# Half-height transposes, 32-column memory products and reciprocal gates in a hand-scheduled segment-attention kernel

## The chip, the cores and the metric

The kernel runs on one core of a Trainium2 chip. The metric is the device time of one execution in microseconds, the median of several runs. The core has a matrix engine (TensorE, "PE" in the profile, its weight loads "PEld"), three elementwise engines (VectorE "DVE", ScalarE "ACT", GpSimd "POOL") and a queue that issues transfers (SyncE, "SP"). PE writes to PSUM, which has banks of 512 float32 a partition; POOL does not touch PSUM here.

## The reference

Per token, the output is a gate g times a segment attention with a compressive memory, plus (1 - g) times x, in which one single token of the sequence gets an FFN added.

```python
# S = 2048 tokens, D = 640, H = 32 heads of 20, 4 segments of L = 512
for s in range(N):
    qs, ks, vs = q[:, :, s], k[:, :, s], v[:, :, s]
    logits = jnp.einsum("bhqd,bhkd->bhqk", qs, ks) * scale + mask      # causal in the segment
    p = _softmax(logits, axis=-1)
    a_dot = jnp.einsum("bhqk,bhkd->bhqd", p, vs)
    pq = phi(qs)
    num = jnp.einsum("bhld,bhde->bhle", pq, M)
    den = jnp.einsum("bhld,bhd->bhl", pq, z)[..., None] + 1e-6
    o = g * (num / den) + (1.0 - g) * a_dot                            # g = sigmoid(beta), per head
    pk = phi(ks)
    M = M + jnp.einsum("bhld,bhle->bhde", pk, vs)
    z = z + jnp.einsum("bhld->bhd", pk)
a = o @ wo
...
return g_x * a + (1 - g_x) * (x + upd)     # g_x = sigmoid(x . gate_w); upd: FFN of the top token
```

## The kernel before

**Staging.** The 32 heads are handled in two halves of 16, each with four segments: eight units `u`. A unit has four groups of four heads, so there are 32 groups `n`. For a unit, five jobs project x to q and k (channels on partitions, jobs 0 to 2) and to v (tokens on partitions, jobs 3 and 4). To keep precision, each operand is a high and a low part, and three products are added. A job is `pair_up`: two PSUM banks are filled at once, one from rows 0 to 63 and one from rows 64 to 127 of the array ("pairs" of matmuls, line L390); in a second phase the two halves are exchanged, and between the phases PE is drained (`where` is then "swap").

**Attention.** q and k go through DRAM (`place`, `place_low`, `bring_back`; L483 and L487 make the high and low parts in rings `hi` and `lo` of two buffers) and come back as stacks `qs`, `ks`. `a_step` makes logits with queries on partitions (L726, mask L733 and L735) for their maxima (L743 on DVE); `b_step` makes them again with keys on partitions (L790), ACT takes the exponential (L794) and POOL the causal select (L800). `pv_step` multiplies with v, with a column of ones for the sum (L815), in four column tiles of 32, one per head; ACT copies the result out (L821). `norm` then transposes it back to tokens on partitions (L842, four transposes of 128x128), divides by the sum and multiplies by `ogate` (DVE, L845 to L848), adds the memory's part (POOL, L851) and stores the rows to DRAM (`otok`).

**Memory.** `memory_read` (L569) multiplies phi(q) of a group with a block matrix `mbd` (80x84), copies the result (ACT, L572), and divides and gates it (DVE L575, L576, POOL L578, L580); there are 24. `memory_write` (L593) makes the update, six times. `keys` (L558) transposes phi(k) in 64-row halves; `m_rows` (L770) transposes the maxima, one small transpose on each half.

**Output stage.** For each of 16 tiles of 128 tokens: `out_rows` loads the rows, transposes them (L1043, five transposes of 128x128 into two banks) and splits them (L1047, L1050), `pair_up` multiplies with `wo`, `out_mix` prepares the x part (ACT L1024 and L1027, POOL L1029), and L1112, L1116 and L1118 finish.

**Order.** Nothing is scheduled by the compiler. The kernel's main loop is a planner that keeps a clock for each engine (`now`), adds an assumed duration with each step (`run`, `pe`, `dma`) and emits the step that comes next. `turned` and `chores` are lists of steps that fit in between: `turn()` runs the first of `turned` when both spare banks are free, `visit()` runs chores, and the product of the next group. Of four banks, two belong to the running pair-up and two (`others()`) are lent out by `misc()`; `flip()` exchanges the pairs. `use(m)` notes the tiling mode of the array, and charges 0.22 us in the planner where it changes: `(64, 128)` for projections, logits, `keys` and `m_rows`, `(128, 32)` for the products with p and the FFN, `(128, 128)` for `norm`, `out_rows`, `memory_read` and `memory_write`. `held` counts, for each high and low copy, the transfers that are not issued yet; `parts_free` lets a next copy begin when the last but one has none left. In this document a "read" is one `memory_read`, an "update" one `memory_write`, and a "visit" a stretch in which PE leaves the 64-row mode and comes back.

## Time and profile before

| | us |
|---|---|
| median of 3 runs | 637.65 |
| lowest, highest | 634.68, 644.41 |
| the profiled execution | 641.31 |
| its span from first to last instruction | 639.6 |

The mean granted clock of PE over the span is 0.98. In the page, "busy" of PE is the union of modelled matmul durations, and these overlap: two matmuls on different halves of the array, or one behind another, lie over each other by part of their length. For what a matmul costs in a stream, the distance from its start to the next one's start is read in the timeline, not its duration. In the timeline a row is a group of like instructions (start, time from the first start to the last end, engine, line, operation, tiles, shapes, count); in the groups a row has count, then total busy time and the mean duration of one in ns, then idle time before. A row of the windows gives the stretch and its length, the busy time and count of PE, PEld, DVE, ACT and POOL, PE's granted clock, DMA's busy share and GB/s. A wait row gives who waited for whom, the total in us, how often, and the longest. A float32 matmul appears as two instructions (eight for the four of a read, 32 for the 16 of an update).

### The profile page before, as it was taken

To read this page: it belongs to the slowest core of one execution; us is meant where nothing else is said; L and a number is where in the kernel's file an instruction comes from. 1 tells how busy PE (TensorE), PEld (TensorE's weight loads), DVE (VectorE), ACT (ScalarE), POOL (GpSimd) and SP (SyncE) were. 2 spreads that over 40 slices of the span, in tenths; PEclk is the share of its full clock that TensorE was granted. 3 is DMA by queue.
4 is the path that set the end of the run, shared out by engine and by line. 5 is a ranking of instruction groups with operands and counts; after the bars stand their busy time and mean duration, and the time that the engine had idled before them with its cause. 6 is when DMAs were issued, how large, how long until landed. Compare 5 with 4: busy or idle time off the path is not lost.

```text
span 639.6 us, 17532 instructions
## 1 busy us (share of the span) xinstructions
PE 599.2 (94%) x7008; PEld 472.4 (74%) x7008; DVE 330.6 (52%) x536; ACT 395.8 (62%) x695; POOL 356.9 (56%) x484
## 2 busy tenths in 40 slices
PE   5998999989999998989999999999999889988996
PEld 4887877777678876767678677786687677766885
DVE  7422555556655545554557465565565565423221
ACT  8736466647667675656766567674666756664442
POOL 4646354544747686647655565664658554554333
PEclk8997999989999999999999999999999979999999
DMA  7797765435554289789868977867465943334451
GB/s 186 221 265 214 203 185 169 133 103 160 136 139 130 77 195 247 226 230 253 271 220 253 259 225 231 235 190 204 149 191 153 271 123 116 95 101 139 145 186 63
DMA packets 81320, 116.57 MB, mean 182 GB/s; under 512 B 36112, under 2 KB 41752, under 8 KB 81240
## 3 DMA queue, kind: packets, MB, share of 16 engines
q1 hardware_dynamic: 81240, 115.46, 62.6%
q8 instruction: 56, 0.92, 0.6%
q14 instruction: 24, 0.20, 0.1%
HBM read 72.94 MB, written 41.96 MB: 180 GB/s over the span
## 4 chain that ended last, share of the span: by engine, by line
PE 78%; DMA 5%; ACT 5%; POOL 3%; DVE 3%; issue 3%; SPq 2%; POOLq 0%; DVEq 0%; ACTq 0%
PE bank L390 41%; PE bank L815 11%; PE a L726 6%; PE bt L790 6%; PE bank L569 3%; PE bank L842 3%; PE bank L593 2%; SPq L151 2%; PE a L735 2%; DMA stkk<-lo 2%; DMA stkq<-hi 1%; PE bank L1043 1%; PE bank L948 1%; DMA ks<-stkk 1%; POOL xf L1029 1%
## 5 line engine op out<-in xcount | busy, mean ns | idle before, releaser
L743 DVE TENSOR_REDUCE mx<-a 128x2 f32<-128x768 f32 (+1 forms) x192 | 160.1, 862 | 111.8 <-PE a L733 59.9
L794 ACT ACTIVATE p<-bt 128x1024 f32<-128x1024 f32 x160 | 163.9, 1025 | 64.3 <-PE bt L790 62.0
L800 POOL TENSOR_SCALAR_AFFINE_SELECT p<-p 128x512 f32<-128x512 f32 (+1 forms) x160 | 87.6, 548 | 105.0 <-ACT p L794 90.0
L390 PE MATMUL bank<-xhi,whi 64*128 64x512 f32 (+1 forms) x480 | 101.7, 386 | 7.7 <-DVE ou L848 3.3
L390 PE MATMUL bank<-xhi,wlo 64*128 64x512 f32 (+1 forms) x480 | 100.6, 377 | 0.0
L390 PE MATMUL bank<-xlo,whi 64*128 64x512 f32 (+1 forms) x480 | 99.1, 371 | 0.6 <-POOL xlo L179 0.6
L790 PE MATMUL bt<-qs,ks 62*128 62x384 f32 (+3 forms) x512 | 74.0, 333 | 4.6 <-ACT p L794 4.6
L726 PE MATMUL a<-ks,qs 60*128 60x384 f32 (+3 forms) x512 | 73.5, 330 | 3.6 <-DMA ks<-stkk 2.5
L815 PE MATMUL bank<-p,va 128*32 128x512 f32 (+3 forms) x1024 | 75.6, 436 | 0.5 <-ACT half L1116 0.4
L390 PEld LDWEIGHTS bank<-xhi,whi 64*128 64x128 f32 x480 | 55.2, 192 | 17.4 <-issue 8.4
L508 POOL TENSOR_TENSOR phi<-phi,neg 128x512 f32<-128x512 f32 x38 | 49.3, 1298 | 24.6 <-ACT phi L506 23.8
L815 PEld LDWEIGHTS bank<-p,va 128*32 128x32 f32 x1024 | 30.0, 109 | 43.9 <-issue 31.0
L487 POOL TENSOR_TENSOR lo<-phi,hi 128x512 fp32r<-128x512 f32 x40 | 51.6, 1293 | 17.0 <-DMA stkk<-lo 16.4
L390 PE MATMUL bank<-whi,xhi 64*128 64x322 f32 (+1 forms) x320 | 58.5, 331 | 2.4 <-DVE fg L937 0.7
L790 PEld LDWEIGHTS bt<-qs,ks 62*128 62x128 f32 x512 | 49.8, 190 | 14.0 <-ACT p L794 5.7
L726 PEld LDWEIGHTS a<-ks,qs 60*128 60x128 f32 x512 | 47.9, 189 | 16.5 <-issue 6.9
L390 PE MATMUL bank<-whi,oh 64*128 64x320 f32 x320 | 52.0, 330 | 7.7 <-DVE ol L1050 6.0
L390 PEld LDWEIGHTS bank<-xlo,whi 64*128 64x128 f32 x480 | 55.8, 192 | 4.5 <-POOL xlo L179 1.0
L390 PEld LDWEIGHTS bank<-xhi,wlo 64*128 64x128 f32 x480 | 56.1, 193 | 3.2 <-issue 0.5
L390 PE MATMUL bank<-wlo,xhi 64*128 64x322 f32 (+1 forms) x320 | 57.2, 320 | 0.0
L390 PE MATMUL bank<-whi,xlo 64*128 64x322 f32 (+1 forms) x320 | 56.5, 315 | 0.0
L821 ACT COPY pvs<-bank 128x512 f32<-128x512 f32 x32 | 18.7, 586 | 58.3 <-PE bank L815 55.1
(121 smaller groups left out, 1142.7 us busy)
## 6 DMA issues: line engine op xcount, KB each, us to landing
qs<-stkq SPq DMA_DIRECT2D x64, 240.0 KB
ks<-stkk SPq DMA_DIRECT2D x64, 240.0 KB
raw<-in_xT_dram SPq DMA_DIRECT2D x40, 256.0 KB
stkq<-hi SPq DMA_DIRECT2D x32, 320.0 KB
stkq<-lo SPq DMA_DIRECT2D x32, 160.0 KB
otok<-ou SPq DMA_DIRECT2D x32, 160.0 KB
xf<-in_x_dram SPq DMA_DIRECT2D x8, 640.0 KB
out_dram<-xf SPq DMA_DIRECT2D x16, 320.0 KB
```

The costliest lines, as they stand in the source:

```text
L390: nc.tensor.matmul(o, a, b, start=phase == 0 and i == 0, stop=phase == 1 and i == n - 1)
L487: nc.gpsimd.tensor_tensor(out=lo, in0=c, in1=f32(hi), op=OP.subtract)
L508: nc.gpsimd.tensor_tensor(out=c, in0=c, in1=r, op=OP.add)
L569: nc.tensor.matmul(nm[:, c, :], e[:GC, 128 * c:128 * c + 128], mbd[:, g, :], start=True, stop=True)
L726: nc.tensor.matmul(a[:, b, at:at + w], q_, ks[n % NS][64 * b:64 * b + ST, p, :w], start=(i, p) == LOGITS[k][0][:2], stop=False)
L743: nc.vector.tensor_reduce(out=mx[n][:, :, p, i:i + 1], in_=a[:, :, at:at + w], axis=AX.X, op=OP.max)
L790: nc.tensor.matmul(bt[:, b, at:at + w], k_, qs[n % NS][64 * b:64 * b + ST + 2, p, L - w:], start=True, stop=True)
L794: nc.scalar.activation(pt, bt, AF.Exp, scale=SCALE)
L800: nc.gpsimd.affine_select(out=d, in_=d, pattern=[[0, e[1]] for e in dims[:-1]] + [[1, 128]], base=0, channel_multiplier=-1, compare_op=OP. ...
L815: nc.tensor.matmul(pv[32 * j:32 * j + 32, 128 * c:], va[u % 2][:, c, VW * h:VW * h + 32], pt_tiles[n, j % 2, c][:, j // 2], start=c == 0, ...
L821: nc.scalar.copy(pvs[n], pv)
L842: nc.tensor.transpose(tp[:, c].rearrange("p j r -> p (j r)"), o[:, 128 * c:128 * c + 128], identf)
```

## The change

- `norm` and `out_rows` transpose in halves of 64 rows into two banks, in mode `(64, 128)`. `norm` is put in `turned` and no longer into `chores`; the next product waits until it has been done.
- `memory_read` and `memory_write` are cut into tiles of 32 output partitions, in mode `(128, 32)`.
- `gate` holds 1 + exp(-beta) and `ogate` 1 + exp(beta), so that a multiplication comes before the one reciprocal.
- `out_mix` uses one DVE instruction where ACT and POOL had one each.
- A next high and low copy begins only when the transfers of the last but one are planned to have landed.
- 22 warm-up transposes stand at the start, 12 before.

```diff
-WARM = 12
+WARM = 22
...
-    held = []
+    held, held_at = [], {}
...
             held[k] -= 1
-            return fn()
+            held_at[k] = max(held_at.get(k, 0.0), fn())
...
     def parts_free():
-        return len(held) < 2 or held[-2] == 0
+        return len(held) < 2 or held[-2] == 0 and held_at[len(held) - 2] <= now["PE"] + 0.3
...
         def fn():
+            nc.scalar.activation(ogate, gate, AF.Exp)
             nc.scalar.activation(gate, gate, AF.Exp, scale=-1.0)
-            nc.vector.tensor_scalar(gate, gate, 1.0, None, op0=OP.add)
-            nc.vector.reciprocal(gate, gate)
-            nc.vector.tensor_scalar(ogate, gate, -1.0, 1.0, op0=OP.mult, op1=OP.add)
...
+            for t in (gate, ogate):
+                nc.scalar.activation(t, t, AF.Copy, bias=1.0)
...
     def memory_read(u, g, e):
-        use((128, 128))
+        use((128, 32))
...
         for c in range(4):
-            nc.tensor.matmul(nm[:, c, :], e[:GC, 128 * c:128 * c + 128], mbd[:, g, :], start=True, stop=True)
-        end = pe(0.6, mbd_at[0])
+            for r in range(0, 128, 32):
+                nc.tensor.matmul(nm[r:r + 32, c, :], e[:GC, 128 * c + r:128 * c + r + 32], mbd[:, g, :], start=True, stop=True)
+        end = pe(0.75, mbd_at[0])
+        rm = pool.tile([128, 4, 4], F32, tag="rm", bufs=2, name="rm")
+        nc.vector.scalar_tensor_tensor(out=rm, in0=nm.rearrange("p c (j e) -> p c j e", e=VW)[:, :, :, DH], scalar=1e-6,
+                                       in1=sub(gate, HH * (u // SEG) + 4 * g, [[0, 4], [1, 4]]), op0=OP.add, op1=OP.mult)
+        mid = run("DVE", 0.25, end)
         t = pool.tile([128, 4, 4, VW], F32, tag="num", bufs=RN, name="num")
         nc.scalar.copy(t.rearrange("p c j e -> p c (j e)"), nm)
-        end = misc_free[i] = run("ACT", 0.55, end)
-        rm = pool.tile([128, 4, 4], F32, tag="rm", bufs=2, name="rm")
-        nc.vector.tensor_scalar(rm, t[:, :, :, DH], 1e-6, None, op0=OP.add)
+        misc_free[i] = run("ACT", 0.55, mid)
         nc.vector.reciprocal(rm, rm)
-        end = run("DVE", 0.5, end)
-        nc.gpsimd.tensor_tensor(out=rm, in0=rm, in1=sub(gate, HH * (u // SEG) + 4 * g, [[0, 4], [1, 4]]), op=OP.mult)
+        end = run("DVE", 0.25)
...
     def memory_write(u):
-        use((128, 128))
+        use((128, 32))
...
             for c in range(4):
-                nc.tensor.matmul(mp[:, g, :], kk[:, g, c, :], va[u % 2][:, c, GW * g:GW * g + GW],
-                                 start=c == 0, stop=c == 3)
-        end = pe(2.3, va_at[0])
+                for r in range(0, GC, 32):
+                    p = slice(r, min(r + 32, GC))
+                    nc.tensor.matmul(mp[p, g, :], kk[:, g, c, p], va[u % 2][:, c, GW * g:GW * g + GW], start=c == 0, stop=c == 3)
+        end = pe(2.6, va_at[0])
...
-        chores.insert(0, (misc_free[i] + 0.1, 0.6, lambda: norm(n), lambda: True))
+        turned.append((misc_free[i] + 0.1, lambda: norm(n), lambda: True))
...
     def norm(n):
-        use((128, 128))
-        tp, i = misc([128, 4, 4, 32])
+        use((64, 128))
...
+        for r in range(2):
+            p = slice(64 * r, 64 * r + 64)
+            tp, i = misc([128, 4, 2, 32])
+            misc_free[i] += 1e6
+            two.append((tp, i, slice(2 * r, 2 * r + 2)))
         for c in range(4):
-            nc.tensor.transpose(tp[:, c].rearrange("p j r -> p (j r)"), o[:, 128 * c:128 * c + 128], identf)
-        end = pe(0.5)
-        rs = pool.tile([128, 4, 4], F32, tag="rs", bufs=2, name="rs")
-        nc.vector.reciprocal(rs, tp[:, :, :, DH])
-        nc.vector.tensor_tensor(out=rs, in0=rs, in1=sub(ogate, HH * hf + 4 * g, [[0, 4], [1, 4]]), op=OP.mult)
-        ou = pool.tile([128, 4, 4, DH], F32, tag="ou", bufs=2, name="ou")
-        nc.vector.tensor_tensor(out=ou, in0=tp[:, :, :, :DH], in1=sub(rs, 0, [[4, 4], [1, 4], [0, DH]]), op=OP.mult)
-        end = misc_free[i] = run("DVE", 1.0, end)
+            for r, (tp, i, h) in enumerate(two):
+                p = slice(64 * r, 64 * r + 64)
+                nc.tensor.transpose(tp[:, c].rearrange("p j r -> p (j r)"), o[p, 128 * c:128 * c + 128], identf[p, p])
+        end = pe(0.47)
+        for tp, i, h in two:
+            nc.vector.tensor_tensor(out=rs[:, :, h], in0=tp[:, :, :, DH], in1=sub(ogate, HH * hf + 4 * g + h.start, [[0, 4], [1, 2]]),
+                                    op=OP.mult)
+        nc.vector.reciprocal(rs, rs)
+        end = run("DVE", 0.6, end)
+        for tp, i, h in two:
+            nc.vector.tensor_tensor(out=ou[:, :, h], in0=tp[:, :, :, :DH], in1=sub(rs, h.start, [[4, 4], [1, 2], [0, DH]]), op=OP.mult)
+            end = misc_free[i] = run("DVE", 0.33)
...
     def out_mix(t):
...
-        row = pool.tile([128, D], F32, tag="raw", bufs=4, name="row")
-        nc.scalar.activation(row, R["yb"], AF.Copy, scale=R["oh"][:, t:t + 1])
-        end = run("ACT", 0.85)
-        nc.gpsimd.tensor_tensor(out=xf[t], in0=row, in1=xf[t], op=OP.add)
-        mixed[t] = run("POOL", 1.6, end)
+        nc.vector.scalar_tensor_tensor(out=xf[t], in0=R["yb"], scalar=R["oh"][:, t:t + 1], in1=xf[t], op0=OP.mult,
+                                       op1=OP.add)
+        mixed[t] = run("DVE", 0.9, end)
...
     def out_rows(t):
-        use((128, 128))
+        use((64, 128))
...
+        for k in range(KT):
+            for r, (tp, i) in enumerate(two):
+                p = slice(64 * r, 64 * r + 64)
+                nc.tensor.transpose(tp[:, k, :], src[k // 4][p, 128 * (k % 4):128 * (k % 4) + 128], identf[p, p])
+        done = pe(0.6, ot_at[t])
+        ready = []
+        for r, (tp, i) in enumerate(two):
+            h_, l_ = (v.rearrange("p (k t) -> p k t", k=KT)[:, :, 64 * r:64 * r + 64] for v in (hi, lo))
+            nc.scalar.copy(h_, tp)
+            end = run("ACT", 0.45, done)
+            nc.vector.tensor_tensor(out=l_, in0=tp, in1=f32(h_), op=OP.subtract)
+            misc_free[i] = run("DVE", 0.5, end)
+            ready = [end + 0.1, misc_free[i] + 0.1]
...
     def pv_ready(t):
-        return n < NG and done_b[0] > n and p_at[n] <= t and misc_ready() <= t
+        return n < NG and done_b[0] > n and n - 1 not in pvs and p_at[n] <= t and misc_ready() <= t
...
     def visit(budget, pv):
-        if pv:
-            if done_pv[0] - 1 in pvs:
-                chores.pop(0)[2]()
...
-        times += [mbd_at[0], step_at[0]] + ...
+        times += [mbd_at[0], step_at[0]] + list(held_at.values())[-2:] + ...
```

More of the change, by code (lines that the diff above doesn't have):

```diff
@@ L426, in fn @@
                 later_dma(end, lambda: bring_back(kind, m), 0.5)
+            return end
         from_part(ready, fn)
@@ L1038, in out_rows @@
         lo = pool.tile([128, D], F32R, tag="lo", bufs=2, name="ol")
-        ready = [], []
-        for k0, k1 in ((0, 4), (4, 5)):
-            tp, i = misc([128, 128 * (k1 - k0)])
-            for k in range(k0, k1):
-                nc.tensor.transpose(tp[:, 128 * (k - k0):128 * (k - k0) + 128], src[k // 4][:, 128 * (k % 4):128 * (k % 4) + 128],
-                                    identf)
-            end = pe(0.13 * (k1 - k0), ot_at[t])
-            c = slice(128 * k0, 128 * k1)
-            nc.scalar.copy(hi[:, c], tp)
-            end = run("ACT", 0.17 + (k1 - k0) / 10, end)
-            ready[0].append(end + 0.1)
-            nc.vector.tensor_tensor(out=lo[:, c], in0=tp, in1=f32(hi)[:, c], op=OP.subtract)
-            misc_free[i] = run("DVE", 0.17 + (k1 - k0) / 7.5, end)
-            ready[1].append(misc_free[i] + 0.1)
+        two = []
+        for r in range(2):
+            tp, i = misc([128, KT, 64])
+            misc_free[i] += 1e6
+            two.append((tp, i))
+        for k in range(KT):
[11 more added lines that the diff above has]
+            ready = [end + 0.1, misc_free[i] + 0.1]
         rowed[t] = hi, lo, ready
@@ L1094, in g @@
                     wh, wl = (v[p, n * b:n * b + n] for v in W["O", k])
-                    return ((h_, wh), (h_, wl), (l_, wh))[part] + (max(ready[part == 2][k == 4], need(("O", k))),)
+                    return ((h_, wh), (h_, wl), (l_, wh))[part] + (max(ready[part == 2], need(("O", k))),)
                 return g
```

10 lines of the change are left out of this document (6 added, 4 removed).

## The prediction

> **What bounds the kernel now.** I read the page first, then the PE timeline around single steps, then the groups and the waits.
>
> ```profile
> span 639.6 us, 17532 instructions
> ...
> PE 599.2 (94%) x7008; PEld 472.4 (74%) x7008; DVE 330.6 (52%) x536; ACT 395.8 (62%) x695; POOL 356.9 (56%) x484
> ...
> PE 78%; DMA 5%; ACT 5%; POOL 3%; DVE 3%; issue 3%; SPq 2%; POOLq 0%; DVEq 0%; ACTq 0%
> PE bank L390 41%; PE bank L815 11%; PE a L726 6%; PE bt L790 6%; PE bank L569 3%; PE bank L842 3%; PE bank L593 2%; SPq L151 2%; PE a L735 2%; DMA stkk<-lo 2%; DMA stkq<-hi 1%; PE bank L1043 1%; PE bank L948 1%; DMA ks<-stkk 1%; POOL xf L1029 1%
> ```
>
> TensorE works for 599.2 of 639.6 us, and 78% of the chain that ended last is its own work, spread over the projections (L390), the products with p (L815), the logits (L726, L790) and, smaller, the three things that the change rewrites: the memory product (L569), the transposes of norm (L842) and the memory update (L593). No other engine is above 62%. So a cut of PE's own time, anywhere, should shorten the run by about the chain's share of it, and work that is moved between ACT, DVE and POOL should matter little except at the end.
>
> **What a change of tiling costs.** The stream runs in 64-row tiles; whenever L842, L569, L593 or L1043 come, the whole array is used, and then the stream returns.
>
> ```profile
> 569.10 0.90 PE L390 MATMUL bank<-whi,ol 64*128 64x320 f32 x10
> 569.92 0.76 PE L1043 MATMUL bank<-identf,ot 128*128 128x128 f32 x5
> 570.62 0.50 PE L790 MATMUL bt<-qs,ks 62*128 62x384 f32 x4
> ...
> 613.22 0.91 PE L390 MATMUL bank<-whi,ol 64*128 64x320 f32 x10
> 614.05 0.77 PE L1043 MATMUL bank<-identf,ot 128*128 128x128 f32 x5
> 614.92 0.41 PE L390 MATMUL bank<-whi,oh 64*128 64x320 f32 x2
> ...
> 616.49 0.90 PE L390 MATMUL bank<-whi,ol 64*128 64x320 f32 x10
> 617.23 0.31 PE L390 MATMUL bank<-whi,oh 64*128 64x320 f32 x2
> ...
> 618.69 0.90 PE L390 MATMUL bank<-whi,ol 64*128 64x320 f32 x10
> 619.68 0.41 PE L390 MATMUL bank<-whi,oh 64*128 64x320 f32 x2
> 619.93 0.31 PE L390 MATMUL bank<-wlo,oh 64*128 64x320 f32 x2
> ...
> 123.09 2.55 PE L593 MATMUL bank<-va,kk 128*80 128x84 f32 x32
> 125.48 0.60 PE L842 MATMUL bank<-identf,pvs 128*128 128x128 f32 x4
> ...
> L842 PE MATMUL bank<-identf,pvs x128: 270/273/330, 94.8 to 584.7; 128*128 128x128 f32 x128
> ```
>
> Ten matmuls (five pairs) take 0.74 us from start to start (616.49 to 617.23), 0.15 a pair. A full transposition of 128x128 takes a step of (0.60 - 0.273) / 3 = 0.109 us. The visit at 569.92 takes 1.52 from the pairs' start to the next matmul; less 0.74 and 5 x 0.109 that leaves 0.24, and the first step after a change is some 0.10 longer (0.25 at 619.68 where 0.15 is usual): 0.34 a visit. Between a pair-up's two phases the code drains PE anyway: without a visit that costs 0.99 - 0.74 = 0.25 (618.69 to 619.68), with one 1.70 - 0.74 - 0.545 = 0.42, so a visit there costs only 0.17.
>
> **Part by part, on PE.**
>
> ```profile
> 107.65 0.22 PE L770 MATMUL bank<-identf,mneg 64*66 64x64 f32 x2
> 107.68 0.48 PE L390 MATMUL bank<-xlo,whi 64*128 64x512 f32 x2
> 107.99 0.39 PE L390 MATMUL bank<-xhi,whi 64*128 64x512 f32 x2
> 108.22 0.39 PE L390 MATMUL bank<-xhi,wlo 64*128 64x512 f32 x2
> ...
> 116.98 0.40 PE L558 MATMUL bank<-identf,phi 64*128 64x64 f32 x4
> ```
>
> Half transposes stand in the trace already. L770 does one on each half at once, inside the stream: 107.65 to 107.99 instead of 0.23, so 0.11 for a pair. L558 does four on one half: (0.40 - 0.22) / 3 = 0.06 a step. Norm becomes four pairs: 0.11 + 3 x 0.06 = 0.29 for 4 x 0.109 = 0.436. 32 x 0.146 = **4.7**. Its worse end, halves one after another, is 0.05 + 8 x 0.06 = 0.53, 3.0 lost. Along the PE timeline 9 of the 32 norms (first at 157.15, last at 584.34) are visits of their own, nearly all at a drain: 9 x 0.17 = **1.5**. The others share theirs with a read, which stays. Output rows: 5 x 0.109 = 0.545 becomes 0.11 + 4 x 0.06 = 0.35; 16 x 0.195 = **3.1** (worse end, 0.05 + 10 x 0.06: 1.7 lost). All 16 visits vanish, 10 in mid-stream and 6 at a drain: 10 x 0.34 + 6 x 0.17 = **4.4**.
>
> ```profile
> 110.65 1.02 PE L569 MATMUL bank<-mbd,phi 80*128 80x84 f32 x8
> ...
> 409.51 2.02 PE L569 MATMUL bank<-mbd,phi 80*128 80x84 f32 x16
> ...
> L569 PE MATMUL bank<-mbd,phi 80*128 80x84 f32 x192 | 25.2, 275 | 0.0
> L569 PEld LDWEIGHTS bank<-mbd,phi 80*128 80x128 f32 x192 | 23.2, 191 | 1.4 <-issue 0.6 <-ACT neg L498 0.4
> ...
> L815 PEld LDWEIGHTS bank<-p,va 128*32 128x32 f32 x1024 | 30.0, 109 | 43.9 <-issue 31.0 <-POOL mneg L758 1.3 <-POOL p L800 0.8
> ...
> 104.36 2.36 PE L815 MATMUL bank<-p,va 128*32 128x512 f32 x32
> 109.16 0.23 PE L733 MATMUL a<-eye,tri 64*128 64x64 bf16 x4
> ```
>
> A memory read is 8 matmuls with a step of (1.02 - 0.275) / 7 = 0.106 and, at 409.51, 0.116: 0.112 taken, 0.90 a read. The update L593 streams the same 84 columns in 2.39 / 32 = 0.075. So a read is bound by its weight load, 0.191 for 128 columns against 0.109 for 32: 0.85 ns a column, 0.109 for 128. With four tiles of 32 columns the load is short; if the four run at once a read takes 8 x 0.075 = 0.60. That they do is in L815: 1280 columns, in two passes for four tiles, one after another at 0.075 / 84 a column, would take 9.1 us, and took 2.36. 24 x 0.30 = **7.2** (worse end: the old step stays, 0; a better one is excluded by the 0.075 of the same columns). The update gets 96 smaller matmuls for 32, three at once: 32 x 0.075 as before, **0**.
>
> Sum on PE: 4.7 + 1.5 + 3.1 + 4.4 + 7.2 = 20.9 us; 78% of it on the chain, **16.3**.
>
> The row that weighs against many small matmuls is L733's: four matmuls of 0.196 to 0.20 us lie in 0.23, so they start some 0.01 apart. The Trainium skill, "TensorE: Matmul & The Clock Gate", section "Wait — 56ns, not 53.3ns?", says that starts never come closer than about 25 ns however small the matmul. By that a read of 32 would take 0.80 and not 0.60, which is the first rival below. The short burst disagrees with it; no row here shows a long stretch.
>
> **Off PE.**
>
> ```profile
> 4.16 2.82 PE L136 MATMUL bank<-identf 128*128 128x128 f32 x12 [4.16 <-DVE identf L129]
> ...
> 11.22 0.63 PE L390 MATMUL bank<-xhi,wlo 64*128 64x512 f32 x2
> 11.65 0.63 PE L390 MATMUL bank<-xlo,whi 64*128 64x512 f32 x2
> ...
> 9.51 3.56 DVE L179 TENSOR_TENSOR xlo<-raw,xhi 128x512 fp32r<-128x512 f32 x3 [0.44 <-ACT xhi L176]
> ...
> 9.00:13.40 4.40, 3.78 (x20) 2.75 (x22) 3.87 (x5) 3.42 (x7) 3.78 (x3) 0.66 0.51 135
> ...
> 230.00:290.00 60.00, 54.53 (x601) 40.27 (x599) 32.69 (x60) 38.78 (x69) 39.49 (x55) 0.97 0.85 229
> ...
> L1029 POOL TENSOR_TENSOR xf<-row,xf 128x640 f32<-128x640 f32 x16 | 25.0, 1565 | 22.3 <-ACT row L1027 20.4 <-ACT mr L772 1.9
> ...
> DVE xf L1112 <- POOL xf L1029: 10.1, 3, 3.9
> POOL lo L487 <- DMA stkk<-lo: 16.4, 4, 7.4
> PE bank L390 <- DVE ou L848: 3.3, 1, 3.3
> ```
>
> Warm-up: 12 transposes take 2.82, 22 about 4.9, ending by 9.1 when real work starts. The stretch 9.0 to 13.4 had a granted clock of 0.66, and a pair took 0.43 for 0.23. A warm array would save up to 8 x 0.2, but waits for the low parts of x, the last of which DVE ends at 13.07; a phase that then has four pairs left ends at 14.0 and not 14.95: **0.9** (ends 0 and 1.6). The same page of the Trainium skill, section "Part 4: PE-mode transpose", says that transposes do not count towards the clock; by that this is 0. Twelve and then two idle microseconds do not tell.
>
> Output mix: POOL's 1.57 and one ACT pass become one DVE pass; DVE waited for POOL there three times, and the last tile is on the chain: **1.0** (ends 0 and 3). The gates: one POOL step less a read, two short DVE steps more a norm; hidden by engines at 52 and 56%, uncovered some 32 x 0.4 = 13 us of DVE. Norm is moved from just ahead of the next product to just behind its own: its DVE steps, POOL's addition and SP's store of the rows come some microseconds earlier, before, not after, what the next reads queue on those engines; the store is waited for only by the output stage, so 0. A read's bank is now freed by a DVE step as well as by ACT's copy: that step stands in DVE's queue behind the maxima, which wait for PE, and a pair-up that needs the bank would wait for it; priced with the bank rival below. The rings: high and low copies no longer stand in ACT's and POOL's queues waiting for a landing, but wait in the planner, with the stacks' DMAs and the return loads on SP behind them. POOL waited 16.4 in four places, PE idled 60 - 54.5 = 5.5 in the stretch where DMA is busiest: **0**, ends 5.5 gained or, should copies be held too long, 5.5 lost.
>
> All: 16.3 + 0.9 + 1.0 = 18.2. The profiled execution took 641.31, so 623.1 in its own time; the median of the three is 637.65, 0.6% lower, which gives 619.4.
>
> **The rivals.**
> - Small matmuls start no closer than 25 ns: a read gains 0.10 instead of 0.30, 24 x 0.20 x 0.78 = 3.7 less: 623. It is the page's rule as a feed limit of this kernel; L733's burst speaks against it. Chance 0.13.
> - The time is given back to ACT and POOL, whose exp and select each cost PE nothing now only because PE is slower: only half of the PE cut (0.4 for 0.78) arrives: 637.65 - 8.4 - 1.9 = 627. For it: DMA share 0.85 and PE idle in 230 to 290; against: 62% of ACT. Chance 0.25.
> - Slower: norm now takes both free banks until five DVE steps end, the next product waits for it, and the next pair-up needs both banks. The one such wait in the trace cost PE 3.3 us. It decides from 18.2 / 32 = 0.57 a norm; at 3.3 in half of the norms it adds 53 and gives 672, at 1.0 a norm 651. Against: one in 32 now, and four short DVE steps more or less. Chance 0.08.
> - The halves do not overlap: 4.7 + 3.0 + 3.1 + 1.7 = 12.5 of PE less, 0.78 of it 9.8: 629. L770's pair speaks against it. Chance 0.04.
>
> **How the numbers follow.** The forecast, 619, has 0.50; its own range is 609 (all of the 20.9 arrives, 4.6 more, and the rings give 5.5) to 627 (the rings cost it, and 2 for scatter of the runs). The range of 607 to 634 takes in the rivals that stay below before, and leaves out the slower one and the tails. Faster by over 2% means under 624.9; 2% is about what this measurement, with runs from 634.68 to 644.41, tells from no change. Forecast 0.45 of 0.50, feed 0.09 of 0.13, giving back 0.06 of 0.25: 0.60. Slower than 650.4: 0.06 from banks, 0.02 for the unforeseen. Within: 0.32.
>
> **What would show it.** L842's and L1043's successors in 64-row form, in pairs with a 0.06 step, and no gaps of 0.34 around them; a read with 32 matmuls in about 0.6 and not 0.8 or 0.9; the update still 2.4; L390 at 0.23 a pair before 13 us if the warm-up works; no POOL or ACT wait for a landing at L487 and L483. I am wrong if PE's busy time falls by less than 15 us, or if it falls and idle time grows by as much, named by a bank or a DVE step of norm.

## The result, and the profile after

| | before | after |
|---|---|---|
| median (us) | 638.03, 4 runs (634.68 to 644.41) | 616.68, 4 runs (615.96 to 617.59) |
| the profiled execution | 641.31 | 617.32 |
| its span | 639.6 | 615.5 |

The ratio is 0.9683, with an interval of 0.9641 to 0.9725: 3.2% faster, 2.3 us below the forecast of 619.0 and inside its range. Executions that lie over 1.5% above the fastest of their kernel, such as the 644.41 here, are left out of the ratios, not of the medians. The profiled execution before lies 3.3 above its median, the one after 0.6, so the 24 us between the two traces stand for 21.4 between the medians. First the page of the kernel after: span, busy time of the engines, and the chain by engine and by line.

```profile
span 615.5 us, 19951 instructions
...
PE 575.3 (93%) x8186; PEld 458.4 (74%) x8186; DVE 335.5 (55%) x614; ACT 386.0 (63%) x682; POOL 326.4 (53%) x443
...
PE 80%; DMA 6%; DVE 3%; ACT 3%; issue 3%; POOL 3%; SPq 1%; POOLq 0%; ACTq 0%; DVEq 0%
PE bank L390 45%; PE bank L819 11%; PE bt L794 6%; PE a L730 6%; PE bank L571 2%; PE bank L598 2%; PE a L739 2%; DMA wt<-in_wg_dram 2%; SPq L151 1%; PE bank L963 1%; PE bank L855 1%; DMA wt<-in_wd_dram 1%; ACT p L798 1%; DMA raw<-in_xT_dram 1%; PE bank L559 1%
```

TensorE's busy time fell by 23.9 us and the span by 24.1, with 1178 more matmuls. The kernel is bound as it was: PE 93%, and its own work 80% of the chain. The old L569, L842 and L1043 are now L571, L855 and L1060 (L593 is L598, L815 is L819, L726 is L730, L790 is L794, L483 and L487 are L484 and L488). Next the PE timeline of the kernel after, one row of each rewritten kind with the rows around it.

```profile
107.09 1.37 PE L571 MATMUL bank<-mbd,phi 80*32 80x84 f32 x64
108.59 0.50 PE L390 MATMUL bank<-xhi,whi 64*128 64x512 f32 x2
...
120.19 0.42 PE L855 MATMUL bank<-identf,pvs 64*128 64x64 f32 x8
120.41 0.38 PE L390 MATMUL bank<-xhi,whi 64*128 64x256 f32 x2
...
122.70 2.52 PE L598 MATMUL bank<-va,kk 128*32 128x84 f32 x96
125.16 0.50 PE L794 MATMUL bt<-qs,ks 62*128 62x256 f32 x4
```

The first row is two reads: 64 matmuls in sixteen sets of four, (1.37 - 0.24) / 15 = 0.075 a set (0.24 is the length of one). The second is a norm: 0.22 from its first transpose to the next matmul of the stream. Over all 32 norms the mean is 8.51 / 32 = 0.27, and it was 17.77 / 32 = 0.56 before (sums from the table below). The third is an update: 96 matmuls in 2.46 (122.70 to 125.16), about as long as the 32 before (2.39, 123.09 to 125.48).

For the whole run I added up, along PE's instructions, the distance from each start to the next start, took out what PE idled, and put each distance to the function in which it begins. "Idle" is PE's idle time between its first and its last matmul; the 4.2 us ahead of the first and the 4.6 to 4.8 behind the last are in "all other". In us:

```
                     before   after
norm                  17.77    8.51    -9.3
memory_read           24.66   16.78    -7.9
out_rows              11.68    7.72    -4.0
memory_write          15.01   14.60    -0.4
warm-up transposes     2.82    4.96    +2.1
projections, L390    321.63  316.61    -5.0
b_step                47.61   44.51    -3.1
pv_step               72.40   74.92    +2.5
all other             94.58   95.49    +0.9
idle                  31.46   31.43     0.0
span                 639.62  615.54   -24.1
```

The rewritten lines (the first four rows) give 21.5 of the 24.1, and PE's idle time is what it was, so in this order of the program nothing of PE's saving was lost to waiting. The idle time stands elsewhere, though: between 120 and 320 us PE idled 11.1 before and 6.2 after, and from 480 us to the end 11.5 before and 15.2 after. Two rows of the waits before, beside the 16.4 of L487 that the prediction shows, and then three of the waits after:

```profile
ACT hi L483 <- DMA stkk<-hi: 6.2, 3, 3.6
...
PE bank L390 <- DVE ol L1050: 6.0, 6, 1.5
```

```profile
POOL lo L488 <- ACT hi L484: 8.9, 9, 2.6
...
PE bank L390 <- DVE ol L1067: 8.3, 7, 2.5
PE bank L1060 <- DMA ot<-otok: 5.1, 1, 5.1
```

The rings' waits for a landing are gone. Waits of the output stage have grown: for the low parts of the rows (L1067), and once for the rows themselves. That single stall is the longest of the run; here is PE's timeline around it, after.

```profile
578.10 0.40 PE L855 MATMUL bank<-identf,pvs 64*128 64x64 f32 x8
...
580.22 0.31 PE L390 MATMUL bank<-wlo,oh 64*128 64x320 f32 x2
580.36 0.90 PE L390 MATMUL bank<-whi,ol 64*128 64x320 f32 x10
586.33 0.71 PE L1060 MATMUL bank<-identf,ot 64*128 64x64 f32 x10 [5.07 <-DMA ot<-otok]
588.12 0.94 PE L390 MATMUL bank<-whi,oh 64*128 64x320 f32 x2 [1.08 <-DVE ol L1067]
...
588.86 0.73 PE L390 MATMUL bank<-whi,oh 64*128 64x320 f32 x2
589.13 0.73 PE L390 MATMUL bank<-wlo,oh 64*128 64x320 f32 x2
```

The last group's norm comes at 578.10, so its rows are stored, loaded again and transposed while PE has nothing else: 5.07 idle. And the work that follows is slow: a pair takes 0.27 (588.86 to 589.13), where 580.22 to 580.36 shows 0.14. The granted clock says why: the mean over the span, before and after, and then windows of the kernel after (stretch and length, busy time of PE, PEld, DVE, ACT, POOL, granted clock, DMA share, GB/s).

```profile
core 0: 639.6 us, clock 0.980
```

```profile
core 0: 615.5 us, clock 0.987
```

```profile
9.00:13.40 4.40, 3.47 (x25) 2.25 (x26) 3.20 (x4) 4.18 (x10) 2.89 (x2) 1.00 0.43 123
230.00:290.00 60.00, 57.84 (x755) 43.74 (x753) 35.41 (x66) 41.04 (x72) 39.59 (x54) 1.00 0.82 248
545.00:560.00 15.00, 12.45 (x134) 8.62 (x134) 3.40 (x9) 4.49 (x9) 4.02 (x6) 0.77 0.30 99
580.00:595.00 15.00, 8.74 (x89) 8.12 (x86) 3.70 (x7) 2.76 (x6) 2.01 (x2) 0.77 0.52 165
```

By its record the clock is granted in full but for stretches at half speed, each 3.41 or 6.83 us long: before at 10.4, 54.8, 129.9, 252.7 and 512.1 us, after at 548.9 and 586.5, each beginning in an idle gap of PE or within 1.5 us of its end (a last one in each run lies behind all matmuls). Missing clock times span is 0.020 x 639.6 = 12.8 us before and 0.013 x 615.5 = 8.0 after. Up to 4.8 of the 24.1 us is therefore clock and not work; less in fact, since some of it falls on idle time. The clock's record begins only at 6.97 us before and at 9.63 after, with a stretch at full clock; the views count what lies ahead of it as 1.00 (more on this below, at the warm-up).

### The profile page after: what moved, and what is told of

It reads as the page before. It is cut to its first block, busy times and chain, and to the rows that moved or that the text cites. A ratio compares the mean times of both kernels' runs of the same rounds, so it can differ in the third digit from the quotient of the medians.

```text
span 615.5 us, 19951 instructions
## 1 busy us (share of the span) xinstructions
PE 575.3 (93%) x8186; PEld 458.4 (74%) x8186; DVE 335.5 (55%) x614; ACT 386.0 (63%) x682; POOL 326.4 (53%) x443
## 4 chain that ended last, share of the span: by engine, by line
PE 80%; DMA 6%; DVE 3%; ACT 3%; issue 3%; POOL 3%; SPq 1%; POOLq 0%; ACTq 0%; DVEq 0%
PE bank L390 45%; PE bank L819 11%; PE bt L794 6%; PE a L730 6%; PE bank L571 2%; PE bank L598 2%; PE a L739 2%; DMA wt<-in_wg_dram 2%; SPq L151 1%; PE bank L963 1%; PE bank L855 1%; DMA wt<-in_wd_dram 1%; ACT p L798 1%; DMA raw<-in_xT_dram 1%; PE bank L559 1%
## 5 line engine op out<-in xcount | busy, mean ns | idle before, releaser
L390 PE MATMUL bank<-xhi,whi 64*128 64x512 f32 (+1 forms) x480 | 99.3, 378 | 2.9 <-ACT xhi L176 0.4
L390 PE MATMUL bank<-xlo,whi 64*128 64x512 f32 (+1 forms) x480 | 97.6, 365 | 0.6 <-POOL xlo L179 0.6
L390 PE MATMUL bank<-xhi,wlo 64*128 64x512 f32 (+1 forms) x480 | 97.7, 367 | 0.0
L819 PE MATMUL bank<-p,va 128*32 128x512 f32 (+3 forms) x1024 | 77.8, 445 | 0.5 <-DVE ou L863 0.5
L730 PE MATMUL a<-ks,qs 60*128 60x384 f32 (+3 forms) x512 | 74.1, 327 | 3.0 <-DVE mx L747 2.7
L794 PE MATMUL bt<-qs,ks 62*128 62x384 f32 (+3 forms) x512 | 73.0, 326 | 3.7 <-ACT p L798 3.7
L390 PEld LDWEIGHTS bank<-xhi,whi 64*128 64x128 f32 x480 | 53.9, 186 | 14.5 <-issue 11.3
L819 PEld LDWEIGHTS bank<-p,va 128*32 128x32 f32 x1024 | 31.1, 111 | 44.5 <-issue 31.7
L390 PE MATMUL bank<-whi,oh 64*128 64x320 f32 x320 | 53.6, 333 | 10.2 <-DVE ol L1067 8.3
L390 PE MATMUL bank<-whi,xhi 64*128 64x322 f32 (+1 forms) x320 | 60.1, 332 | 1.8 <-issue 0.3
L488 POOL TENSOR_TENSOR lo<-phi,hi 128x512 fp32r<-128x512 f32 x40 | 51.7, 1294 | 13.6 <-ACT hi L484 8.9
L390 PE MATMUL bank<-wlo,xhi 64*128 64x322 f32 (+1 forms) x320 | 58.6, 320 | 0.0
L390 PEld LDWEIGHTS bank<-xlo,whi 64*128 64x128 f32 x480 | 55.0, 186 | 4.5 <-POOL xlo L179 1.4
L794 PEld LDWEIGHTS bt<-qs,ks 62*128 62x128 f32 x512 | 49.5, 186 | 11.6 <-ACT p L798 4.6
L390 PE MATMUL bank<-whi,xlo 64*128 64x322 f32 (+1 forms) x320 | 57.7, 313 | 0.0
L730 PEld LDWEIGHTS a<-ks,qs 60*128 60x128 f32 x512 | 48.6, 186 | 11.3 <-issue 4.6
L390 PEld LDWEIGHTS bank<-xhi,wlo 64*128 64x128 f32 x480 | 54.7, 186 | 2.6 <-issue 0.2
```

The source lines that it names most:

```text
L390: nc.tensor.matmul(o, a, b, start=phase == 0 and i == 0, stop=phase == 1 and i == n - 1)
L488: nc.gpsimd.tensor_tensor(out=lo, in0=c, in1=f32(hi), op=OP.subtract)
L730: nc.tensor.matmul(a[:, b, at:at + w], q_, ks[n % NS][64 * b:64 * b + ST, p, :w], start=(i, p) == LOGITS[k][0][:2], stop=False)
L794: nc.tensor.matmul(bt[:, b, at:at + w], k_, qs[n % NS][64 * b:64 * b + ST + 2, p, L - w:], start=True, stop=True)
L819: nc.tensor.matmul(pv[32 * j:32 * j + 32, 128 * c:], va[u % 2][:, c, VW * h:VW * h + 32], pt_tiles[n, j % 2, c][:, j // 2], start=c == 0, ...
```

## The experiments

Twelve kernels ran. In three sets of runs the kernel before had medians of 638.0, 641.9 and 638.6 (the second is 637.4 without its three runs of 643.8 to 645.6), so the ratio is the better number for comparisons; that of the change itself is 0.9683, with an interval of 0.9641 to 0.9725. An edit that only changes instructions inside a step keeps the planner's order; one that changes an assumed duration, a bank or a condition gives another order of the whole program. The first two kernels below keep the order of the kernel that they start from, and so do those with 12 warm-up transposes, with halves in turn and with dummies; the others do not.

**The read alone, taken out of the change.**

```diff
-            for r in range(0, 128, 32):
-                nc.tensor.matmul(nm[r:r + 32, c, :], e[:GC, 128 * c + r:128 * c + r + 32], mbd[:, g, :], start=True, stop=True)
+            nc.tensor.matmul(nm[:, c, :], e[:GC, 128 * c:128 * c + 128], mbd[:, g, :], start=True, stop=True)
```

> The changed kernel with the memory read alone back in four full-height products a read (8 matmuls); the planner's order, modes and durations stay as in the changed kernel, so every other instruction stands where it stood. The changed kernel has a median of 616.7. If all of PE's time arrives in the span: 24 x (0.90 - 0.60) = 7.1 more, and about 0.14 for each of some 6 reads that now stand beside a 32-column block: 624.6. If only the chain's share of 78% arrives: 622.9. If the read's time was covered: 617. In the trace a read has 8 matmuls with a step of 0.11.

Measured: 632.95 (629.98 to 634.1), ratio 0.9907 (0.9867 to 0.9947), so 16.3 us are lost, 8.3 more than the 624.6 expected. PE's timeline at the place of the two reads shown above, in this kernel:

```profile
107.00 2.02 PE L570 MATMUL bank<-mbd,phi 80*128 80x84 f32 x16
109.12 0.50 PE L390 MATMUL bank<-xhi,whi 64*128 64x512 f32 x2
```

Two reads with their visit take 2.12 and not 1.50: 0.31 a read, near the 0.30 of the prediction. Over the run `memory_read` is 26.0 for 16.8, so 9.2 of the 15.8 that the span grew. PE's idle time has 1.6 of the rest (33.1 for 31.4); the other 5 lie on lines whose instructions are the same. The clock's mean is 0.976, so 0.024 x 631.3 = 15.2 are missing, 7.2 more than with the change, which could explain them. Six half-speed stretches lie on its work for two, three of them (191.9, 222.6 and 256.8 us) after gaps of PE of 0.6 to 1.0 us; gaps of that size stand in the kernel after as well, and none of these cost it any clock.

**The read alone, put into the kernel before.** The same lines, the other way round.

> The kernel before with the memory read alone in 32-column tiles; modes and durations of the planner stay, so the order is that of before. By the step sizes 24 x (0.90 - 0.60) = 7.1 less if all arrives, 5.6 at the chain's share: 638.0 to 631 or 632.4. If matmuls started no closer than 25 ns, 2.3 less: 636. A read then also changes mode against the norm beside it, some 15 x 0.14 = 2 more: 633 and 634.5.

Measured: 636.52 (10 runs, 634.52 to 639.16), ratio 0.9990 (0.9952 to 1.0029). In the profiled run the span is 634.3, 5.3 shorter; `memory_read` takes 18.1 for 24.7, but `norm` 19.2 for 17.8: with the read in 32-column tiles and the transposes in full ones, the two no longer share a visit. So the read's cut is 6.5 on its own line, 5.1 with its neighbour. The times show none of it for certain: the medians differ by 2.0, and the interval takes in 1. The traces differ by more because the profiled execution of the kernel before lies 3.3 above its median (clock 0.980) and that of this kernel 0.6 below its own (clock 0.988), which is 3.8 of the 5.3. That the tiles gain more once norm has left the 128-row mode is what the lines say; by the times it is not shown.

**Norm alone, taken out:** four transposes of 128x128 into one bank, and the DVE steps on whole tiles.

```diff
-        use((64, 128))
+        use((128, 128))
+        tp, i = misc([128, 4, 4, 32])
...
-                nc.tensor.transpose(tp[:, c].rearrange("p j r -> p (j r)"), o[p, 128 * c:128 * c + 128], identf[p, p])
+            nc.tensor.transpose(tp[:, c].rearrange("p j r -> p (j r)"), o[:, 128 * c:128 * c + 128], identf)
```

> The changed kernel with norm alone back in four full transposes into one bank, in its new place in the order, with the gate's reciprocal form kept (one DVE product, one reciprocal, one product). The prediction's terms (steps 4.7, visits 1.5) give 622.9 if all arrives, 621.5 at 78%. But here each of the 32 norms stands by itself in the 64-row stream, so that up to 32 visits at 0.17 to 0.34 are paid and not 9: 616.7 + 4.7 + 5.4 to 10.9 = 627 to 632. If the banks held by two-bank norms were what limits, it would be faster than 616.7.

Measured: 618.41 (618.12 to 619.02), ratio 0.9698 (0.9666 to 0.9730): 1.7 us lost by the medians, where 627 to 632 was expected; the interval overlaps that of the change. `norm` takes 18.8 for 8.5, so 10.3 came back on PE; but PE idles 23.1 for 31.4, and there is no stall like the one at 586. The order is another, and the last store of rows comes at 564.7 us, where the kernel after has it at 581.2. What the step saves on PE is seen again; what it is worth in time can't be read from this run.

**The output rows alone, taken out:** five transposes of 128x128 in two parts.

```diff
-        use((64, 128))
+        use((128, 128))
...
-                nc.tensor.transpose(tp[:, k, :], src[k // 4][p, 128 * (k % 4):128 * (k % 4) + 128], identf[p, p])
+                nc.tensor.transpose(tp[:, 128 * (k - k0):128 * (k - k0) + 128], src[k // 4][:, 128 * (k % 4):128 * (k % 4) + 128],
+                                    identf)
```

> The changed kernel with the output rows alone back in five full transposes of 128x128. The prediction's terms (steps 3.1, visits 4.4) give 624.2 if all arrives. If the output stage is bound by something else than PE (the rows' way through DRAM after the last product, DVE's low part before the next pair-up), 616.7 to 620.

Measured: 611.82 (610.26 to 617.62), ratio 0.9622 (0.9565 to 0.9679): 4.9 us *faster* by the medians than with the whole change, though one of the four runs took 617.62 and the intervals overlap a little. `out_rows` takes 11.6 for 7.7, as expected, yet PE idles 23.2 for 31.4 and the clock is 0.997. Two rows of the wait view of this kernel:

```profile
PE bank L390 <- DVE ol L1063: 5.5, 6, 1.5
...
PE bt L794 <- ACT p L798: 3.3, 4, 1.0
```

The wait for the low parts is 5.5 and not 8.3, the wait of 5.1 for the rows is not there (the last store comes at 572.4), and with the gaps went both half-speed stretches; one of 3.41 stands at 188.8 instead. (The second row, a wait for the exponential, is the next longest.) So the new form of the rows saves 3.9 on PE and, in the order of the kernel after, seems to give back more. One of its costs is its own: with halves of rows a pair-up's low product needs all of the low parts, where the old form let it begin with the first four blocks. How much is that and how much the order, these runs don't separate.

**The warm-up alone, taken out** (22 back to 12).

```diff
-WARM = 22
+WARM = 12
```

> The changed kernel with 12 warm-up transposes for 22, nothing else. If transposes release the clock: the granted clock falls back to about 0.66 in the stretch 9.0 to 13.4 and the time rises by 0.9 (prediction) to 1.7 (half a clock for 3.4 us): 617.6 to 618.4. If they do not count, as the page of the Trainium skill says, nothing changes: 616.7, and the granted clock of that stretch is 1.00 for another reason.

Measured: 624.17 (620.97 to 630.75; 621.27 without the run of 630.75), ratio 0.9785 (0.9719 to 0.9852): 4.6 to 7.5 us lost, with an interval that just touches that of the change. The start, in PE's timeline, of this kernel and then of the kernel after:

```profile
4.16 2.82 PE L136 MATMUL bank<-identf 128*128 128x128 f32 x12 [4.16 <-DVE identf L129]
9.20 0.80 PE L390 MATMUL bank<-xhi,whi 64*128 64x512 f32 x2 [2.21 <-ACT xhi L176]
...
11.57 0.63 PE L390 MATMUL bank<-xhi,wlo 64*128 64x512 f32 x2
12.00 0.62 PE L390 MATMUL bank<-xlo,whi 64*128 64x512 f32 x2
...
14.91 0.50 PE L390 MATMUL bank<-xhi,whi 64*128 64x512 f32 x2
```

```profile
4.16 4.96 PE L136 MATMUL bank<-identf 128*128 128x128 f32 x22 [4.16 <-DVE identf L129]
9.48 0.56 PE L390 MATMUL bank<-xhi,whi 64*128 64x512 f32 x2 [0.37 <-ACT xhi L176]
...
11.41 0.39 PE L390 MATMUL bank<-xhi,wlo 64*128 64x512 f32 x2
11.64 0.40 PE L390 MATMUL bank<-xlo,whi 64*128 64x512 f32 x2
...
14.42 0.50 PE L390 MATMUL bank<-xhi,whi 64*128 64x512 f32 x2
```

And the window of this start, with 12:

```profile
9.00:13.40 4.40, 4.07 (x20) 2.82 (x22) 3.49 (x5) 4.20 (x11) 2.87 (x2) 1.00 0.51 147
```

With 12 a pair takes 0.43 up to 12.4 us (11.57 to 12.00); with 22 it takes 0.23 from 11 us on. The 1.00 in this row does not mean that the clock was granted in full: the clock's record of this run begins at 12.74 us, and the view counts what lies ahead of it as full. The pairs turn fast just where the record begins, in all three kernels that show it: 0.43 until 12.4, 13.6 and 14.3 us, with records that begin at 12.74 (this kernel), 13.57 (the guard alone) and 14.58 (the read alone, on the kernel before). And 0.43 is what a pair takes in a recorded half-speed stretch too: in the kernel before, from 10.8 to 13.4 us, inside the stretch at 10.38. So the slow start is the half clock. With 22 transposes the record begins between 7.5 and 10.1 us in all ten kernels that have them.

The second phase starts at 14.42 with 22 and at 14.91 with 12: the warm-up is worth 0.5 us there, and 0.8 against the trace of the kernel before (15.21). The rest of what was lost has no one place. In the profiled run, 3.7 longer in span, PE idles 2.3 more (33.7 for 31.4), and the missing clock is 0.016 x 619.3 = 9.9 for 8.0, with half-speed stretches at 190.2, 541.8, 555.5 and 589.6 us.

**Halves one after another in the program**, for norm and rows, to see what the interleaving does.

```diff
-        for c in range(4):
-            for r, (tp, i, h) in enumerate(two):
+        for r, (tp, i, h) in enumerate(two):
+            for c in range(4):
...
-        for k in range(KT):
-            for r, (tp, i) in enumerate(two):
+        for r, (tp, i) in enumerate(two):
+            for k in range(KT):
```

> The changed kernel with the halves of norm and of the output rows one after the other (all four, or five, transposes of the upper half, then those of the lower) instead of in pairs; every other instruction and the order as in the changed kernel. If pairs run at once, as read from the trace of before, undoing that costs 4 x 0.06 a norm and 5 x 0.06 an output tile: 32 x 0.24 + 16 x 0.3 = 12.5 on PE, of which the output tiles' part may be hidden: 617 + 8 to 12 = 625 to 629. If the halves never overlapped, nothing changes: 617.

Measured: 618.44 (616.22 to 621.98), ratio 0.9687 (0.9606 to 0.9768): no different from the change. A norm in its PE timeline:

```profile
119.51 0.41 PE L855 MATMUL bank<-identf,pvs 64*128 64x64 f32 x7
119.73 0.36 PE L390 MATMUL bank<-xhi,whi 64*128 64x256 f32 x1
119.76 0.23 PE L855 MATMUL bank<-identf,pvs 64*128 64x64 f32 x1
119.80 0.36 PE L390 MATMUL bank<-xhi,whi 64*128 64x256 f32 x1
```

All eight start within 0.25 us (119.51 to 119.76), whichever way the program has them, as if each half of the array had a queue of its own. So the edit didn't make them serial, and the expectation built on it fell with it. The time alone would also fit halves that never overlap; the timeline rules that out, since eight steps of 0.06 one after another would take 0.48. Whether PE does this or what lies between the program and the engine, no run here tells.

**The array kept busy through the tail stall:** 64 dummy pairs of transposes ahead of the rows of tile 12, overwritten afterwards.

```diff
+        if t == 12:
+            for _ in range(64):
+                for r, (tp, i) in enumerate(two):
+                    p = slice(64 * r, 64 * r + 64)
+                    nc.tensor.transpose(tp[:64, 0, :], identf[p, p], identf[p, p])
```

> The changed kernel with 64 pairs of transposes of a constant, about 4 us of PE work whose result is overwritten, just ahead of the transposes of output tile 12, where PE stands idle for 5.07 us at 581 to 586 in the trace; order as in the changed kernel. If an idle gap costs its length and then up to 6.8 us at half clock, and transposes count as activity, the half-clock stretch at 586.5 goes and the run is up to 3.4 shorter: 613.3. If transposes do not count, the stretch stays and the time is 616.7 to 617.5.

Measured: 620.30 (619.32 to 621.04), ratio 0.9732 (0.9654 to 0.9810). Its PE timeline there:

```profile
582.60 3.74 PE L1061 MATMUL bank<-identf 64*64 64x64 f32 x128
587.83 0.46 PE L1065 MATMUL bank<-identf,ot 64*128 64x64 f32 x8 [1.50 <-DMA ot<-otok]
589.42 0.28 PE L1065 MATMUL bank<-identf,ot 64*128 64x64 f32 x2 [1.12 <-DMA ot<-otok]
590.82 0.89 PE L390 MATMUL bank<-whi,oh 64*128 64x320 f32 x2 [1.13 <-DVE ol L1072]
```

The dummies cover 3.7 us; gaps of 1.50, 1.12 and 1.13 remain, and a half-speed stretch still begins at 591.2, of 3.41 us for 6.83. That idling less shortened it is not shown: the stretch after the gap of 2.47 at 547 us in the kernel after, which the edit does not touch, also takes 3.41 here (at 553.7) for 6.83 there. Nothing was gained in all, against the 613.3 hoped for: two more stretches (188.5 and 437.6 us) came in the same run.

**The rings' guard**, taken out of the change, and put alone into the kernel before.

```diff
-        return len(held) < 2 or held[-2] == 0 and held_at[len(held) - 2] <= now["PE"] + 0.3
+        return len(held) < 2 or held[-2] == 0
...
-        times += [mbd_at[0], step_at[0]] + list(held_at.values())[-2:] + [e[1]
+        times += [mbd_at[0], step_at[0]] + [e[1]
```

> The changed kernel with the old guard of the high and low rings (transfers issued, not landed). The prediction gave the guard 0 with ends of 5.5: 611 to 622. If the guard is worth something, waits of ACT at the high copy and of POOL at the low copy for landings come back (16.4 and 6.2 in the trace of before) and PE's idle time rises with them.

> The kernel before with the guard of the rings alone. If what the changed kernel lost without it (628.8 for 616.7) is the guard's own work, waiting in the planner and not in ACT's and POOL's queues, this is about 12 faster: 626. If that loss came from the order that the planner happened to find, this lies anywhere within some 10 of 638, and the waits for landings (16.4 of POOL at the low copy, 6.2 of ACT at the high one) go without the time following.

Measured: without it 628.76 (625.84 to 632.23), ratio 0.9872 (0.9771 to 0.9973), 12 us lost; alone on the kernel before 634.74 (10 runs, 632.10 to 638.33), ratio 0.9947 (0.9913 to 0.9982), 3.4 us gained. The wait view of the change without it:

```profile
POOL lo L488 <- ACT hi L484: 15.0, 8, 9.0
...
ACT hi L484 <- DMA stkk<-hi: 6.1, 3, 2.8
...
PE bank L1060 <- DMA ot<-otok: 5.0, 1, 5.0
```

The wait for a landing is back on ACT (6.1), POOL waits 15.0 behind it for 8.9, and PE idles 36.7 for 31.4. On the kernel before, PE idles 27.9 for 31.5. Both point to a gain: 3.6 of PE's idle time alone, 5.3 when taken out. But both also have another order, and an order alone moves PE's idle time by 4 to 7 (next experiment), so how much is the guard's own is not shown. The 12 did not come back on the kernel before; what else is in them was not taken apart.

**The order alone.** `KEEP` is the rest of a pair-up's phase, in us of PE, below which the planner lends no spare bank to a step that comes between. No instruction is added or removed; they are only put in another order. 1.2 became 1.0, and in another kernel 1.4.

```diff
-KEEP = 1.2
+KEEP = 1.0
```

> The changed kernel with the planner's reserve before the end of a pair-up (KEEP) at 1.0 and not 1.2: the same instructions in another order. Its own clock ends at 584.6 where the changed kernel's ends at 600.5. If order alone moves the time by more than 2%, the time falls to 600 to 610; if the planner's clock tells nothing of the chip's, 612 to 622.

> The changed kernel with KEEP at 1.4 and not 1.2: the same instructions in another order, not chosen for speed; the planner's clock ends at 597.8 for 600.5. With KEEP at 1.0 (609.2) it gives the size of what order alone does. If order is worth little here, 615 to 618; if single undos were moved by their order as much as by their content, it differs from 616.7 by 5 or more, either way.

Measured: with 1.0 609.21 (605.25 to 610.24), ratio 0.9533 (0.9446 to 0.9621); with 1.4 623.55 (621.05 to 627.22), ratio 0.9795 (0.9711 to 0.9878). One and the same work lies 14 us apart. PE idles 24.6 with 1.0, 31.4 with 1.2 and 35.4 with 1.4, which is the difference of the spans (608.5, 615.5, 619.4) to within 0.2. The longest wait of PE in each, with 1.4 and then with 1.0:

```profile
490.91 0.80 PE L730 MATMUL a<-ks,qs 60*128 60x256 f32 x4 [9.03 <-DVE mx L747]
```

```profile
PE bank L390 <- DVE ol L1067: 7.0, 4, 3.4
```

With 1.0 the last rows are stored at 561.3 us, early enough that the tail has no stall. It is the fastest kernel of this study by its median, faster than the kernels before and after; its interval does not touch that of the change. No run says that 1.0 is better in general. The old form of the rows together with it was not tried.

**The planner told the truth.** Its assumed durations of five steps were set to those measured.

```diff
-        end = pe(0.75, mbd_at[0])
+        end = pe(0.6, mbd_at[0])
...
-        end = pe(2.6, va_at[0])
+        end = pe(2.4, va_at[0])
...
-        end = pe(2.05, p_at[n])
+        end = pe(2.25, p_at[n])
...
-        end = pe(0.47)
+        end = pe(0.29)
...
-        done = pe(0.6, ot_at[t])
+        done = pe(0.35, ot_at[t])
```

> The changed kernel with five planner durations set to what the trace shows: norm 0.29 for 0.47, read 0.6 for 0.75, update 2.4 for 2.6, output rows 0.35 for 0.6, product with p 2.25 for 2.05; same instructions. The planner's clock ends at 586.7 for 600.5. If a truer clock gives a better order, 600 to 612; if it does not matter, 612 to 622.

Measured: 618.50 (616.07 to 620.95), ratio 0.9700 (0.9617 to 0.9784), no different from the change. PE idles 27.3, 4 less, but the clock fell to 0.979. Truer durations alone gave no faster kernel here.

## Why the prediction was right, point by point

- **What bounds it.** PE's own time: its busy time fell by 23.9, the span by 24.1. Right.
- **How much arrives.** The prediction let 78% of PE's cut through, the chain's share. In this order all of it did: idle time is 31.4 in both, where the step had 4.6 lost. The traces lie 5.8 from the forecast in the profiled run's terms (623.1 for 617.32), the medians 2.3. How much of that belongs to this step stays open: up to 4.8 is clock, and PE's idle time was 24.6 or 35.4 with the same instructions in another order (KEEP at 1.0 and 1.4), so 31.4 in both is partly chance. A share of the chain says how much of the end is PE's now, not how much of a saving is lost; and what the rings' guard and the missing norm stall took out of the middle (the 3.3 after L848 is gone) was put back at the end by the output stage.
- **Norm.** 4.7 and 1.5 foreseen, 9.3 measured on its lines, 10.3 when it was taken out. Only 0.8 of the 3.1 between them is in the new norm, at 0.27 for the 0.29 priced (8.51 for 9.28; the single one shown takes 0.22). The other 2.3 is in the old one, which cost 17.77 and not 32 x 0.436 + 1.5 = 15.5. In PE's timeline before, a norm took 0.49 where a read followed in the same visit and 0.66 where it stood alone at a drain; 0.436 and 0.61 had been taken. So it was the old norm that was mis-sized: the change took more away than was priced.
- **Output rows.** 3.1 and 4.4 foreseen. 4.0 measured on the lines themselves (3.9 when taken out). Before, these lines took 11.68 / 16 = 0.73 a tile, 0.185 over the 0.545 of the transposes, so 3.0 of the visits' cost lay on them; after, 7.72 / 16 = 0.48 for the 0.35 priced, which takes 2.1 back. The new form was mis-sized there. What else the visits cost lies in L390, whose -5.0 also holds clock, and wasn't measured by itself. Not foreseen: the wider wait for low parts (8.3 for 6.0) and the tail stall. The run without this part is the faster one by its median.
- **Reads and updates.** 7.2 foreseen, 7.9 measured on the lines, 9.2 when taken out, 6.5 when put alone into the kernel before (5.1 with norm's lost companion). Updates 0 foreseen, 0.4 measured.
- **The start.** 0.9 foreseen, 0.5 measured at the second phase against 12 transposes, 0.8 against the trace of the kernel before. The Trainium skill, "TensorE: Matmul & The Clock Gate", section "Part 4: PE-mode transpose", has transposes not count towards the clock. The traces disagree: before, the record of full clock begins at 6.97 us, when PE had run nothing but the twelve transposes since 4.16, and with ten more the pairs take 0.23 where they took 0.43.
- **Guard.** 0 was taken, with ends of 5.5 either way: 3.4 gained alone, in another order, and in the stretch of 230 to 290 us, on which the ends rested, PE idles 60 - 57.8 = 2.2 for 5.5. The value was too low if that gain is the guard's own; it lies inside the ends either way.
- **Output mix.** 1.0 foreseen. The wait of 10.1 at L1112 for POOL's L1029 is gone with that step, but it wasn't tried alone, and its worth stays open.
- **Rivals.** The feed limit of 25 ns (the same page of the Trainium skill, section "Wait — 56ns, not 53.3ns?") is refuted for this kernel: four matmuls in 0.075, 19 ns each, over 64 of them. The time given back to ACT and POOL did not come: PE's idle time did not grow. The bank stall did not come: PE waited 1.1 us in all for L863, a norm's last DVE step, at L571 and L819. The halves do overlap, 0.06 a pair.
- **What was missing.** The half-speed stretches and the order. Each moves the time by as much as a term of the sum: up to 4.8 us for the one, -7.5 to +6.9 for the other. That the total came within 2.3 us is partly luck: in the kernel drawn both were of moderate size, and norm, sized too low, and output rows, sized too high on their lines, offset each other. The parts taken out one by one, +16.3, +1.7, -4.9, +7.5 and +12, add up to 32.6, more than the 21.4 of the whole, and no sum of the parts can be made of them.

## What to carry to other kernels

Price work on a busy matrix engine by the distance from one start to the next, in its own tiling mode, with the two changes of mode added: that gave 7.2 us for the reads, and 7.9 was measured. The sum, 20.9 for 21.5 on the rewritten lines, agrees better than its terms do: norm had 6.2 for 9.3, and the output rows 7.5 for 4.0 on their lines. Price the old form as carefully as the new one. In a program whose order a planner makes, an edit also draws another order: judge an edit by its own lines and the idle time apart, and compare times only where the order is kept, or over several orders. Look at where the last loads depend on late steps, because an idle gap there costs its own length and then the clock of what follows.

## What the runs showed of the hardware

- The granted clock falls to one half for 3.41 us or a multiple (6.83, 10.24 and 13.65 also occur) around idle gaps of PE. Gaps of 2 us and more mostly have one; gaps of 0.6 to 1.0 us had one in the kernel with the read taken out and none in the kernel after, which has the same order.
- A window's granted clock of 1.00 says nothing of the time ahead of the clock's first record. With 12 warm-up transposes pairs took 0.43 us up to 12.4 us in a window shown as 1.00; the record of that run begins at 12.74.
- Transposes alone brought the full clock: the record before begins at 6.97 us, after 2.8 us of transposes and nothing else on PE.
- Four fp32 matmuls of 84 columns on four column tiles take 0.075 us from one set of four to the next (19 ns a matmul, over 64), and an update of 96 small ones takes about as long as one of 32 (2.46 and 2.39).
- Transposes written as four on the upper half and then four on the lower ran side by side, all eight in 0.25 us.
